# Inputs of an attention laid out as [d, token], the keys' maximum as a bias, and a new order of the attention's pieces

## The chip, the core and the metric

The kernel runs on one core of a Trainium2 chip. A core has five engines with a queue each: TensorE (PE; its weight loads are listed as PEld), VectorE (DVE), ScalarE (ACT), GpSimd (POOL) and SyncE (SP), which here issues all transfers. TensorE writes to PSUM; the others work on SBUF, and all but GpSimd also on PSUM. The metric is the device time of one execution in microseconds (us), lower is better.

## The reference

For 4 batches of 8 heads, 576 tokens and 64 dimensions per head, an attention with positive features, and then two feed-forward layers on the 2304 tokens:

```python
def phi(x):
    proj = np.einsum('bhsd,df->bhsf', x, w_phi)                      # 128 features
    proj = proj - np.max(np.abs(proj), axis=-1, keepdims=True)
    return np.concatenate([np.exp(proj), np.exp(-proj)], axis=-1)
q_p, k_p = (phi(q), phi(k))
kv = np.einsum('bhsf,bhsd->bhfd', k_p, v)
z = np.sum(k_p, axis=2)
num = np.einsum('bhsf,bhfd->bhsd', q_p, kv)
den = np.einsum('bhsf,bhf->bhs', q_p, z)[..., None] + 1e-06
attn = num / den
# x: the heads side by side, [2304, 512]
h = x @ w_in;    x = (h * sigmoid(h)) @ w_out          # 512 -> 2048 -> 512
h = x @ w2_in;   out = (h * np.cos(h)) @ w2_out
```

As the code computes it, the exponentials are exp(proj - max) and exp(-(proj - max)), where max is taken over the absolute values. The weights of the feed-forward layers are float64.

## The kernel before

Most products are made of float32 numbers split into two parts of fewer bits, hi and lo, and three matmuls: hi with hi, hi with lo, lo with hi. "Split" below means a cast to the short format (hi) and a subtraction (lo, the rest).

**The attention** works on eight groups n of four heads. Its pieces, as the tables START and PERIOD (L49, L55) name them:

- `load.k`, `load.q`, `load.v`: transfers. For k and q a main load of 512 KB and two small ones for the last 64 tokens of each head (the tails).
- `T.k.i`, `T.q.i` (L270, `transpose_in`): TensorE transposes a piece of k or q, [token, d], into PSUM (tile `tp`, two buffers); ScalarE casts it out of PSUM to hi, VectorE subtracts for lo.
- `phi.k.u`, `phi.q.u` (L290): products with w_phi into PSUM (tile `p`, two buffers); VectorE takes the maximum of absolute values (L304, `m`) and subtracts it (L306, `pm`, in SBUF). Unit 0 is the tails of the four heads, units 1 to 4 a head each.
- `kx.u` (L311): two exponentials on ScalarE, of +pm and -pm, for the keys.
- `qx.u` (L319): TensorE transposes pm of the queries (tile `t`, one buffer); ScalarE takes both exponentials (`e`), GpSimd casts them to hi (`qh`, L338).
- `ql.u.g` or `ql.u.v` (L341): the rest of the queries' exponentials, on GpSimd or VectorE.
- `kv.p.c.h` (L350): products of the keys' features with v and a column of ones; at the end ScalarE and VectorE split the sums. `num.p.i` (L373): the queries' features with these sums; ScalarE copies the result to `xn`.
- `inv.p` (L179): the inverses of the denominators, through a transfer to DRAM and back. `app.p` (L191): numerators times inverses, to x (`xy`), three multiplications on GpSimd.
- `piece`: a step of the conversion of a float64 weight (L99 to L126: a ScalarE step, three VectorE steps, two GpSimd steps for each of the first six weight tiles). `x`: x of the first tokens is split for the first layer.

Engines take their queues in the order in which the code issues them: the loop over n (L446) runs through PERIOD once per group, and a + or - at a piece's name shifts it by one group. One run through PERIOD is called a round here; the queries of a group meet the keys of the next one in it.

**The feed-forward layers** (L477, `moe`): for each layer, four groups of hidden columns by six blocks of 384 tokens, with the remaining weights converted beside the products. The change doesn't touch them, but for the row order of tokens in `store` (L567).

Of the kernel before, what the change touches and what calls it, by code (L numbers as in the profile page):

```python
# [158 lines left out]
class Norm:  # L159
    """Numerators over denominators, to x, [dm, token]."""  # L160
# [30 lines left out]
    def apply(self, n, p):  # L191
        nc, xy = self.nc, self.xy
# [7 lines left out]
        nc.gpsimd.tensor_mul(xy[rows, B * NJ + b // 2, c0:c0 + 2, at], t[rows, :, SM:S], r[rows, :, SM:S])  # L200


def attention(tc, q, k, v, w_phi, norm, pieces, then):
    nc = tc.nc
    W = D + 1
    with ExitStack() as ctx:
# [5 lines left out]
        kr, krt, qr, qrt = {}, {}, {}, {}  # L212

        def load_qk(n, src, main, tails, name):
            b, h0 = divmod(n, 2)
            h0 *= 4
            t = fp.tile([P, 4, NJ, D], F32, name=f"{name}r")
            u = fp.tile([P, 2, D], F32, name=f"{name}rt")
            for i in range(2):
                nc.sync.dma_start(u[64 * i:64 * i + 64], src[b, h0 + 2 * i:h0 + 2 * i + 2, SM:S, :].rearrange("h s d -> s h d"))  # L220
            nc.sync.dma_start(t, src[b, h0:h0 + 4, 0:SM, :].rearrange("h (p j) d -> p h j d", j=NJ))
            main[n], tails[n] = t, u
# [480 lines left out]
```

## Time and profile before

| | |
|---|---|
| median of 3 runs (lowest, highest) | 1051.86 us (1050.23, 1052.01) |
| span of the profiled execution, first to last instruction | 1048.8 us |
| busy in the span | PE 97%, DVE 68%, ACT 39%, POOL 35% |
| first product of the feed-forward layers | 228.6 us |
| starts of five rounds after another | 43.9, 71.8, 100.0, 128.4, 156.2 us |
| loads of k (512 KB), from issue to landing | 4.3 us (median) |
| loads of q (512 KB), from issue to landing | 4.1 us (median) |

The profiled execution's own time is not listed among the runs; its span is 3.1 us below their median. The shares are means over an attention of some 229 us and feed-forward layers of some 820 us, so the stretches have to be read apart. A round's start is taken here at the longest row of `kv` products (L363, 16 matmul rows), which stands once in each round.

### The profile page before, as it was taken

To read this page: it belongs to the slowest core of one execution; us is meant where nothing else is said; L and a number is where in the kernel's file an instruction comes from. 1 tells how busy PE (TensorE), PEld (TensorE's weight loads), DVE (VectorE), ACT (ScalarE), POOL (GpSimd) and SP (SyncE) were. 2 spreads that over 40 slices of the span, in tenths; PEclk is the share of its full clock that TensorE was granted. 3 is DMA by queue.
4 is the path that set the end of the run, shared out by engine and by line. 5 is a ranking of instruction groups with operands and counts; after the bars stand their busy time and mean duration, and the time that the engine had idled before them with its cause. 6 is when DMAs were issued, how large, how long until landed. Compare 5 with 4: busy or idle time off the path is not lost.

```text
span 1048.8 us, 15083 instructions
## 1 busy us (share of the span) xinstructions
PE 1019.1 (97%) x6000; PEld 972.5 (93%) x6000; DVE 711.9 (68%) x956; ACT 407.8 (39%) x664; POOL 369.4 (35%) x426
## 2 busy tenths in 40 slices
PE   7999999999999999999999999999999999999998
PEld 7989999989999999999999999899888988998997
DVE  6999999978544344544545567667677867786764
ACT  5655566544433222222223333444333333333332
POOL 3566666656122111201211024334434433343221
PEclk9999999999999999999999999999999999999999
DMA  4544333114111101110110111101110111100112
GB/s 118 139 112 112 99 105 81 47 40 129 41 41 46 55 22 61 41 41 21 61 48 34 41 41 42 40 21 61 41 41 21 61 40 41 27 34 1 61 57 63
DMA packets 62757, 58.33 MB, mean 56 GB/s; under 512 B 30560, under 2 KB 55264, under 8 KB 62688
## 3 DMA queue, kind: packets, MB, share of 16 engines
q1 hardware_dynamic: 62688, 57.38, 18.5%
q8 instruction: 47, 0.77, 0.3%
q14 instruction: 22, 0.18, 0.1%
HBM read 52.49 MB, written 4.79 MB: 55 GB/s over the span
## 4 chain that ended last, share of the span: by engine, by line
PE 61%; DVE 25%; POOL 7%; ACT 4%; issue 1%; DMA 1%; SPq 0%; POOLq 0%; ACTq 0%; DVEq 0%
PE h L509 24%; PE y L558 6%; PE y L560 6%; PE y L559 6%; DVE ql L346 4%; DVE tb L531 3%; DVE tb L530 3%; DVE tb L535 3%; PE kv L363 3%; POOL ta L529 2%; PE y L563 2%; PE y L564 2%; PE y L565 2%; DVE xy L589 2%; POOL gh L536 2%; DVE gl L538 2%
## 5 line engine op out<-in xcount | busy, mean ns | idle before, releaser
L509 PE MATMUL h<-xh,win_hi 128*128 128x384 f32 x768 | 259.1, 337 | 1.7 <-DVE tb L535 1.7
L509 PE MATMUL h<-xl,win_hi 128*128 128x384 f32 x768 | 258.8, 337 | 0.3 <-DVE xl L474 0.3
L509 PE MATMUL h<-xh,win_lo 128*128 128x384 f32 x768 | 258.7, 337 | 0.0
L521 DVE SCALAR_TENSOR_TENSOR ta<-ta,h 128x768 f32<-128x768 f32 x48 | 45.8, 953 | 177.7 <-ACT ta L520 177.7
L509 PEld LDWEIGHTS h<-xh,win_hi 128*128 128x128 f32 x768 | 144.2, 188 | 4.7 <-PE y L565 2.6
L509 PEld LDWEIGHTS h<-xl,win_hi 128*128 128x128 f32 x768 | 144.2, 188 | 2.4 <-DVE xl L474 0.6
L509 PEld LDWEIGHTS h<-xh,win_lo 128*128 128x128 f32 x768 | 144.2, 188 | 0.0
L532 ACT ACTIVATE tb<-tb 128x768 f32<-128x768 f32 x48 | 40.7, 847 | 239.0 <-DVE tb L531 239.0
L558 PE MATMUL y<-gh,wout_hi 128*128 128x384 f32 x384 | 129.5, 337 | 0.2 <-ACT xy L587 0.2
L560 PE MATMUL y<-gh,wout_lo 128*128 128x384 f32 x384 | 129.6, 337 | 0.0
L559 PE MATMUL y<-gl,wout_hi 128*128 128x384 f32 x384 | 129.4, 337 | 0.0
L520 ACT ACTIVATE ta<-h 128x768 f32<-128x768 f32 x48 | 39.0, 813 | 206.4 <-PE h L509 203.1
L563 PE MATMUL y<-wout_hi,gh 128*128 128x512 f32 x288 | 115.0, 399 | 3.3 <-ACT xy L587 1.8
L564 PE MATMUL y<-wout_lo,gh 128*128 128x512 f32 x288 | 114.4, 397 | 0.0
L565 PE MATMUL y<-wout_hi,gl 128*128 128x512 f32 x288 | 114.4, 397 | 0.0
L536 POOL TENSOR_SCALAR gh<-tb 128x768 fp32r<-128x768 f32 x48 | 46.9, 977 | 186.0 <-DVE tb L535 176.0
L538 DVE TENSOR_TENSOR gl<-tb,gh 128x768 fp32r<-128x768 f32 x48 | 75.4, 1570 | 34.3 <-POOL gh L536 34.3
L121 POOL TENSOR_SCALAR wout_hi<-wt 128x512 fp32r<-128x512 f32 x32 | 27.8, 869 | 200.3 <-DVE wt L118 171.1
L121 POOL TENSOR_SCALAR win_hi<-wt 128x512 fp32r<-128x512 f32 x32 | 21.6, 675 | 187.1 <-DVE wt L118 187.1
L589 DVE TENSOR_TENSOR xy<-y,xy 128x384 f32<-128x384 f32 (+1 forms) x126 | 70.8, 606 | 9.7 <-PE y L560 6.0
L535 DVE TENSOR_TENSOR tb<-tb,h 128x768 f32<-128x768 f32 x48 | 45.6, 951 | 46.7 <-ACT tb L533 46.2
L558 PEld LDWEIGHTS y<-gh,wout_hi 128*128 128x128 f32 x384 | 72.1, 188 | 0.5 <-ACT xy L587 0.5
(114 smaller groups left out, 2082.6 us busy)
## 6 DMA issues: line engine op xcount, KB each, us to landing
raw<-in_moe_w_in SPq DMA_DIRECT2D x32, 512.0 KB, 3.6
raw<-in_moe_w_out SPq DMA_DIRECT2D x32, 512.0 KB, 3.6
rb<-rd SPq DMA_DIRECT2D x16, 288.0 KB, 3.6
kr<-in_k SPq DMA_DIRECT2D x8, 512.0 KB, 4.3
qr<-in_q SPq DMA_DIRECT2D x8, 512.0 KB, 4.1
va<-in_v SPq DMA_DIRECT2D x32, 128.0 KB, 4.1
out<-xy SPq DMA_DIRECT2D x16, 256.0 KB, 2.2
krt<-in_k SPq DMA_DIRECT2D x16, 32.0 KB, 3.1
```

Of the source, the lines that this page charges most:

```text
L121: nc.gpsimd.tensor_scalar(hi, t.bitcast(F32), 1.0, 0.0, op0=ALU.mult, op1=ALU.add)
L509: nc.tensor.matmul(o, a[:, cs], x[t][:, :, c, :], start=first, stop=(c == NC - 1 and a is lo))
L535: nc.vector.tensor_mul(b, b, h)
L536: nc.gpsimd.tensor_scalar(hi, b, 1.0, 0.0, op0=ALU.mult, op1=ALU.add)
L538: nc.vector.tensor_sub(lo, b, hi.bitcast(F32))
L558: nc.tensor.matmul(o, wh[:, ds], hi[:, f, :], stop=False, **st)
L559: nc.tensor.matmul(o, wh[:, ds], lo[:, f, :], start=False, stop=False)
L560: nc.tensor.matmul(o, wl[:, ds], hi[:, f, :], start=False, stop=en)
L563: nc.tensor.matmul(o, hi[:, f, ds], wh, stop=False, **st)
L564: nc.tensor.matmul(o, hi[:, f, ds], wl, start=False, stop=False)
L565: nc.tensor.matmul(o, lo[:, f, ds], wh, start=False, stop=en)
L589: nc.vector.tensor_tensor(y, o, y, op=ALU.add)
```

## The change

- **Layout.** k and q reach the device as one array of 8 groups, [64 dimensions of two heads, tokens], tails first. One load of 576 KB per group takes the place of three. The transposes of the inputs and their tiles in PSUM are gone; `sp.k.i`, `sp.q.i` split the inputs straight from SBUF: a cast on the engine that the table names (D VectorE, A ScalarE, G GpSimd) and the rest on VectorE.
- **Keys.** VectorE still takes the maximum of `p`. GpSimd writes its negative (`nm`, 4 or 2 columns). ScalarE takes the exponentials out of PSUM, with `nm` and `m` as bias per token, 128 columns at a time: 8 (tail: 4) instructions instead of 2. VectorE's subtraction for the keys is gone; the tile `p` in PSUM is held until the exponentials are done.
- **Other engines.** The casts of the queries' exponentials go from GpSimd to ScalarE (two of them go to VectorE and two stay, in START). `ql.1` goes from VectorE to GpSimd, `app.1` from GpSimd to VectorE.
- **Buffers in PSUM.** `p` has three (was two), `t2` two (was one; `tp` had two).
- **Order.** START and PERIOD are rewritten. Tokens are assigned to tiles as j*128 + p instead of p*4 + j, which moves the rows of v's loads and of the output's stores.

The paths under `FULL`, an empty tuple, are not taken.

```diff
+PB, T2, KN = 3, 2, 3
 PERIOD = parse("""
-kx.1+ x.2+ num.1.1 x.3+ phi.k.2+ T.k.0++ phi.q.0+ num.1.0 x.4+ load.q++ kx.2+ num.1.2 x.5+ kv.0.0.0+ inv.0 phi.k.0++
...
+ql.4.D num.0.1 x.2+ num.0.2 num.0.3 kx.0+ num.1.0 kx.2+ sp.q.0.D+ x.4+ phi.k.3.A+ num.1.1 piece inv.0 num.1.2
...
         def load_qk(n, src, name):
+            t = fp.tile([P, GC], F32, name=f"{name}r")
+            nc.sync.dma_start(t, src[n])
...
-        def transpose_in(n, name, i):
...
-                    nc.tensor.transpose(ps[:, c * P:(c + 1) * P], src, ident)
...
-            nc.scalar.copy(hi, ps)
-            nc.vector.tensor_sub(lo, ps, hi.bitcast(F32))
...
+        def split_in(n, name, i, engine):
+            at = slice(0, P + SM) if i == 0 else slice(P + SM, GC)
+            hi, lo = xT[n, name, i] = [fp.tile([P, at.stop - at.start], F32R, name=f"{name}T_{part}{i}") for part in ("hi", "lo")]
+            src = raw[n, name][:, at]
+            cast(engine, hi, src)
+            nc.vector.tensor_sub(lo, src, hi.bitcast(F32))
...
             nc.vector.tensor_reduce(m, pv, axis=AX.X, op=ALU.max, apply_absolute_value=True)
+            if engine == "A":
+                nm = sp.tile([P, 2 * ns], F32, name="nm", bufs=3)
+                nc.gpsimd.tensor_scalar(nm, m, -1.0, 0.0, op0=ALU.mult, op1=ALU.add)
+                if name == "k":
+                    pm[n, name, u] = pv, m, nm
+                    return
...
-            nc.scalar.activation(t[:, 0], src, AF.Exp)
-            nc.scalar.activation(t[:, 1], src, AF.Exp, scale=-1.0)
+            for i in range(ns if m is not None else 0):
+                nc.scalar.activation(t[:, 0, i], src[:, i], AF.Exp, bias=nm[:, i:i + 1])
+                nc.scalar.activation(t[:, 1, i], src[:, i], AF.Exp, bias=m[:, i:i + 1], scale=-1.0)
...
-                    nc.gpsimd.tensor_scalar(hi, ev, 1.0, 0.0, op0=ALU.mult, op1=ALU.add)
+                        cast(engine, hi, ev)
...
-            nc.gpsimd.tensor_mul(xy[rows, b * NJ:(b + 1) * NJ, c0 + x, :], t[rows, x, 0:SM].rearrange("p (j n) -> p j n", n=P),
+            engine.tensor_mul(xy[rows, b * NJ:(b + 1) * NJ, c0 + x, :], t[rows, x, 0:SM].rearrange("p (j n) -> p j n", n=P),
```

Three places show how the instructions stand. VectorE before, in the middle of a round; `ql` are the rests of the queries, `m` a maximum, `pm` its subtraction, `wt` a weight, `r` the inverses:

```order
L346 TENSOR_TENSOR ql0_1896<-e_1955,qh0_1895 128x512
L346 TENSOR_TENSOR ql0_1896<-e_1958,qh0_1895 128x512
L183 TENSOR_SCALAR r_1993<-den_1890 128x9
L184 RECIPROCAL r_1993<-r_1993 128x9
L304 TENSOR_REDUCE m_2006<-p_1999 128x4
L306 TENSOR_TENSOR pm_2008<-p_1999,m_2006 128x512
L368 TENSOR_TENSOR kv0_lo_128<-kv_1846,kv0_hi_127 128x260
L118 SCALAR_TENSOR_TENSOR wt_1909<-ws_1907,wt_1909 128x512
L346 TENSOR_TENSOR ql0_1896<-e_1985,qh0_1895 128x512
L346 TENSOR_TENSOR ql0_1896<-e_1988,qh0_1895 128x512
```

VectorE now, at the end of a round and the start of the next; `xy` are multiplications of x, `qT_hi` and `qT_lo` the split of q:

```order
L397 TENSOR_TENSOR kv0_lo_122<-kv_1358,kv0_hi_121 128x260
L307 TENSOR_REDUCE m_1570<-p_1566 128x2
L374 TENSOR_TENSOR ql1_1408<-e_1541,qh1_1407 128x512
L374 TENSOR_TENSOR ql1_1408<-e_1542,qh1_1407 128x512
L397 TENSOR_TENSOR kv1_lo_124<-kv_1417,kv1_hi_123 128x4x65
L307 TENSOR_REDUCE m_1624<-p_1617 128x4
L205 TENSOR_TENSOR xy_63<-xn1_1295,rb_1340 64x4x128 x2
L208 TENSOR_TENSOR xy_63<-xn1_1295,rb_1340 64x2x64
L374 TENSOR_TENSOR ql1_1408<-e_1581,qh1_1407 128x512
L374 TENSOR_TENSOR ql1_1408<-e_1582,qh1_1407 128x512
L280 CAST qT_hi0_1691<-qr_1428 128x640
L290 TENSOR_TENSOR qT_lo0_1692<-qr_1428,qT_hi0_1691 128x640
```

Two of the round's rests, its multiplications of x, the last rests and the first split of q now stand close together, with only maxima and `kv_lo` between them; before, maxima with their subtractions, the inverses and a weight stood between two of the rests. On GpSimd, before, one round from the first casts of the queries' exponentials (`qh`) on:

```order
L338 TENSOR_SCALAR qh0_1101<-e_1161 128x512
L338 TENSOR_SCALAR qh0_1101<-e_1164 128x512
L197 TENSOR_TENSOR xy_63<-xn0_898,rb_1063 64x4x128 x2
L200 TENSOR_TENSOR xy_63<-xn0_898,rb_1063 64x2x64
L338 TENSOR_SCALAR qh0_1101<-e_1191 128x512
L338 TENSOR_SCALAR qh0_1101<-e_1194 128x512
L121 TENSOR_SCALAR win1_hi_66<-wt_1115 128x512
L338 TENSOR_SCALAR qh1_1103<-e_1229 128x512
L338 TENSOR_SCALAR qh1_1103<-e_1232 128x512
L338 TENSOR_SCALAR qh1_1103<-e_1251 128x512
L338 TENSOR_SCALAR qh1_1103<-e_1254 128x512
L197 TENSOR_TENSOR xy_63<-xn1_998,rb_1063 64x4x128 x2
```

GpSimd now, from the maximum of the keys' unit 4 on, where the code has `phi.k.4` (`nm` are the negated maxima, `win` a weight):

```order
L310 TENSOR_SCALAR nm_1439<-m_1437 128x4
L374 TENSOR_TENSOR ql0_1406<-e_1450,qh0_1405 128x512
L374 TENSOR_TENSOR ql0_1406<-e_1451,qh0_1405 128x512
L205 TENSOR_TENSOR xy_63<-xn0_1222,rb_1340 64x4x128 x2
L208 TENSOR_TENSOR xy_63<-xn0_1222,rb_1340 64x2x64
L129 TENSOR_SCALAR win2_hi_68<-wt_1331 128x512
L134 TENSOR_TENSOR win2_lo_69<-wt_1331,win2_hi_68 128x512
L310 TENSOR_SCALAR nm_1556<-m_1554 128x4
L310 TENSOR_SCALAR nm_1572<-m_1570 128x2
L310 TENSOR_SCALAR nm_1626<-m_1624 128x4
L310 TENSOR_SCALAR nm_1704<-m_1702 128x4
```

The casts of the queries' exponentials are gone from it; two rests of 512 columns, one set of multiplications of x and a weight stand in one piece, and the negated maxima of the keys' units 1, 0 and 2 behind it. On ScalarE, before, the exponentials of a group's queries (`e`, `et`) out of PSUM:

```order
L332 ACTIVATE et_1502<-t2_1495 128x256
L332 ACTIVATE et_1506<-t2_1495 128x256
L103 ACTIVATE ws_1510<-raw_720 128x512
L332 ACTIVATE e_1558<-t2_1553 128x512
L332 ACTIVATE e_1561<-t2_1553 128x512
L332 ACTIVATE e_1588<-t2_1583 128x512
L332 ACTIVATE e_1591<-t2_1583 128x512
L367 CAST kv0_hi_127<-kv_1449 128x260
```

ScalarE now, in the same place:

```order
L366 ACTIVATE e_1123<-t2_1118 128x512
L278 CAST qh0_1020<-e_1123 128x512
L366 ACTIVATE e_1124<-t2_1118 128x512
L278 CAST qh0_1020<-e_1124 128x512
L366 ACTIVATE e_1156<-t2_1151 128x512
L278 CAST qh1_1022<-e_1156 128x512
L366 ACTIVATE e_1157<-t2_1151 128x512
L278 CAST qh1_1022<-e_1157 128x512
L395 CAST kv0_hi_121<-kv_973 128x260
```

Behind each exponential stands the cast of its result.

## Rows read from the trace of the kernel before

**Rows 1.** Busy time by stretch: from:to, its us, each engine's busy us (instructions), clock, DMA.
```profile
0.00:8.10 8.10, 1.98 (x8) 1.72 (x9) 1.34 (x5) 1.94 (x3) 2.69 (x22) 1.00 0.46 127
0.00:228.62 228.62, 208.54 (x1680) 205.42 (x1681) 210.52 (x339) 133.94 (x298) 135.38 (x206) 0.97 0.36 96
128.43:156.23 27.80, 25.94 (x212) 25.83 (x212) 27.27 (x45) 16.62 (x37) 18.15 (x26) 0.94 0.39 106
156.23:182.60 26.37, 24.36 (x205) 23.93 (x205) 25.50 (x42) 15.81 (x37) 17.00 (x23) 1.00 0.36 91
260.00:1048.80 788.80, 779.73 (x4151) 737.06 (x4149) 476.78 (x592) 260.32 (x348) 218.45 (x207) 1.00 0.13 41
```

**Rows 2.** Line 346, attention: count, duration ns min/median/max, first and last start.
```profile
L346 DVE TENSOR_TENSOR ql<-e,qh x62: 677/922/2987, 26.4 to 226.5; 128x512 fp32r<-128x512 f32 x62
```

**Rows 3.** Timeline of VectorE, one round: start us, us, line, operation, tiles, shapes.
```profile
132.69 3.78 DVE L346 TENSOR_TENSOR ql<-e,qh 128x512 fp32r<-128x512 f32 x2
...
146.94 0.28 DVE L285 TENSOR_TENSOR kT_lot<-tp,kT_hit 128x128 fp32r<-128x128 f32 x1
...
148.46 1.33 DVE L346 TENSOR_TENSOR ql<-e,qh 128x512 fp32r<-128x512 f32 x2
149.71 0.68 DVE L285 TENSOR_TENSOR qT_lom<-tp,qT_him 128x512 fp32r<-128x512 f32 x1
150.31 0.67 DVE L304 TENSOR_REDUCE m<-p 128x4 f32<-128x512 f32 x1
151.02 0.69 DVE L306 TENSOR_TENSOR pm<-p,m 128x512 f32<-128x512 f32 x1
```

**Rows 4.** Timeline of GpSimd, same round.
```profile
132.55 2.50 POOL L197 TENSOR_TENSOR xy<-xn,rb 64x512 f32<-64x512 f32 x2
...
147.35 1.29 POOL L126 TENSOR_TENSOR win_lo<-wt,win_hi 128x512 fp32r<-128x512 f32 x1
```

**Rows 5.** VectorE's groups, 0 to 229 us: count, busy us, mean ns, idle before.
```profile
L346 DVE TENSOR_TENSOR ql<-e,qh 128x512 fp32r<-128x512 f32 x62 | 70.5, 1178 | 0.2 <-POOL qh L338 0.2
...
L306 DVE TENSOR_TENSOR pmt<-p,m 128x256 f32<-128x256 f32 x16 | 6.8, 424 | 0.5
...
L107 DVE TENSOR_SCALAR wt<-raw 128x512 int32<-128x512 int32 x6 | 2.7, 442 | 0.0
```

**Rows 6.** GpSimd's groups, 0 to 229 us.
```profile
L338 POOL TENSOR_SCALAR qh<-e 128x512 fp32r<-128x512 f32 x64 | 44.2, 711 | 11.7 <-ACT e L332 11.6
L197 POOL TENSOR_TENSOR xy<-xn,rb 64x512 f32<-64x512 f32 x28 | 40.6, 1468 | 1.9 <-DMA rb<-rd 1.5
...
L346 POOL TENSOR_TENSOR ql<-e,qh 128x512 fp32r<-128x512 f32 x2 | 2.5, 1278 | 0.0
```

**Rows 7.** Timeline of TensorE at the start.
```profile
6.56 1.97 PE L278 MATMUL tp<-ident,kr 128*128 128x128 f32 x8 [2.14 <-DMA kr<-in_k]
8.18 0.56 PE L299 MATMUL p<-wphi,kT_hit 128*128 128x256 f32 x1
```

**Rows 8.** Timeline of TensorE in that round; in brackets the idle time before.
```profile
138.64 1.09 PE L324 MATMUL t<-ident,pm 128*128 128x128 f32 x4 [1.86 <-DVE pm L306]
...
149.00 0.60 PE L278 MATMUL tp<-ident,kr 128*128 128x128 f32 x4
149.35 0.37 PE L299 MATMUL p<-wphi,qT_hit 128*128 128x256 f32 x1
```

**Rows 9.** ScalarE's groups, 0 to 229 us.
```profile
L315 ACT ACTIVATE kp<-pm 128x512 f32<-128x512 f32 x32 | 20.3, 634 | 8.5 <-DVE pm L306 8.3
...
L284 ACT CAST kT_him<-tp 128x512 fp32r<-128x512 f32 x16 | 9.4, 589 | 5.4 <-PE tp L278 5.2
...
L315 ACT ACTIVATE kpt<-pmt 128x256 f32<-128x256 f32 x8 | 3.4, 425 | 1.5 <-DVE pmt L306 1.5
...
L284 ACT CAST kT_hit<-tp 128x128 fp32r<-128x128 f32 x8 | 2.1, 265 | 2.5 <-PE tp L280 2.4
```

**Rows 10.** Busy time and granted clock just behind TensorE's wait.
```profile
138.00:142.00 4.00, 3.36 (x19) 3.39 (x20) 3.96 (x7) 1.48 (x3) 2.49 (x3) 0.58 0.35 97
```

More of the change, by code (lines that the diff above doesn't have):

```diff
@@ L210, in attention, with load_qk @@
         pp = ctx.enter_context(tc.tile_pool(name="at_ps", bufs=1, space=PSUM))
[L212 to L222, printed above, removed]
+        raw = {}
+        def load_qk(n, src, name):
+            t = fp.tile([P, GC], F32, name=f"{name}r")
+            nc.sync.dma_start(t, src[n])
+            raw[n, name] = t
         def load_v(n):
@@ L255, in attention @@
                 nc.gpsimd.memset(t[64 * x:64 * x + 64, i % 2, c:c + 1], 1.0)
-        kvs = [[sp.tile([P, 2, 2, M], F32R, name=f"kv{i}_{part}") for part in ("hi", "lo")] for i, M in enumerate((W, P))]
+        kvs = [[sp.tile([P, 2, 2, M], F32 if i in FULL else F32R, name=f"kv{i}_{part}") for part in (("all",) if i in FULL else ("hi", "lo"))]
+               for i, M in enumerate((W, P))]
         for t in kvs[1]:
@@ new lines, in attention, with cast @@
+        engines = {"D": nc.vector, "A": nc.scalar, "G": nc.gpsimd}
+        def cast(engine, out, src):
+            if engine == "A":
+                nc.scalar.copy(out, src)
+            elif engine == "D":
+                nc.vector.tensor_copy(out, src)
+            else:
+                nc.gpsimd.tensor_scalar(out, src, 1.0, 0.0, op0=ALU.mult, op1=ALU.add)
+        def split_in(n, name, i, engine):
[4 more added lines that the diff above has]
+            nc.vector.tensor_sub(lo, src, hi.bitcast(F32))
@@ new lines, in q_exp @@
+            for i in full:
+                for c in range(2):
+                    src = ps[:, i, :].rearrange("p (x s) -> p x s", x=2) if u == 0 else ps.rearrange("p a s -> p (a s)")
+                    nc.scalar.activation(qh[n, i][:, c, :, SM:S] if u == 0 else qh[n, i][:, c, x, 0:SM], src, AF.Exp, scale=1.0 - 2.0 * c)
+            parts = rests[n, u] = []
+            if u and full or len(full) == 2:
+                return
+            es = [sp.tile([P, ns, P], F32, name="et" if u == 0 else "e", bufs=2 if u == 0 else 4) for _ in range(2)]
@@ L341, in q_rest @@
         def q_rest(n, u, engine):
-            for c in range(2):
-                for i in range(2 if u == 0 else 1):
-                    lo, ev, hi = rests.pop((n, u, c, i))
-                    engine.tensor_sub(lo, ev, hi.bitcast(F32))
+            for _, ev, hi, lo in rests.pop((n, u)):
+                engine.tensor_sub(lo, ev, hi.bitcast(F32))
         kvp = {}
@@ L402, in step @@
                 return then(front)
-            key = (n, name, *arg)[:3] if name == "ql" else (n, name, *arg)
+            key = (n, name, *(a for a in arg if a not in engines))
             if key in done or not 0 <= n < NQ:
@@ L424, in step @@
             elif name == "ql":
-                q_rest(n, arg[0], nc.gpsimd if arg[1] == "g" else nc.vector)
+                q_rest(n, arg[0], engines[arg[1]])
             elif name == "kv":
@@ L439, in step @@
             elif name == "app":
-                norm.apply(n, *arg)
+                norm.apply(n, arg[0], engines[arg[1]])
         done.update({(0, "load", "k"), (0, "load", "q")})
@@ L692 @@
     for name in ("q", "k", "v", "w_phi", "moe_w_in", "moe_w_out", "moe2_w_in", "moe2_w_out"):
-        a = np.ascontiguousarray(inputs[name])
+        a = inputs[name]
+        if name in ("q", "k"):
+            x = np.asarray(a).reshape(2 * B, 4, S, D)
+            main = x[:, [0, 2, 1, 3], :SM].reshape(2 * B, 4, 2, 2, P, D).transpose(0, 3, 5, 1, 2, 4).reshape(2 * B, P, 8 * P)
+            tail = x[:, :, SM:].reshape(2 * B, 2, 2, S - SM, D).transpose(0, 2, 4, 1, 3).reshape(2 * B, P, P)
+            a = np.concatenate([tail, main], axis=2)
+        a = np.ascontiguousarray(a)
         if a.dtype == np.float64:
```

121 lines of the change are left out of this document (64 added, 57 removed).

## The prediction, written before the changed kernel ran

> **What bounds the kernel now.** I cut the span into stretches first, then read one round of the attention in the timelines, then the groups of instructions. The busy shares of the whole span are means over two parts with different limits. From 260 us to the end TensorE is busy for 779.7 of 788.8 us: the two feed-forward layers are TensorE's, and the change leaves their work as it is (only the order of the output rows differs) [rows 1]. The attention is the other part: the first product of the feed-forward layers starts at 228.6 us, and up to there VectorE is busy for 210.5 us [rows 1]. In one round (128.43 to 156.23 us) VectorE is busy for 27.27 of 27.80 us, TensorE for 25.94, ScalarE for 16.62, GpSimd for 18.15 [rows 1]. So a round is as long as VectorE's list, with TensorE close behind and ScalarE at 60%.
>
> Why VectorE's list is that long is the main reading. The same instruction, the rest of the queries' exponentials (L346, 128x512, both inputs in SBUF), takes from 677 to 2987 ns [rows 2]. Two of them take 1.33 us where GpSimd is almost idle, and 3.78 us where it multiplies x beside them [rows 3, 4]. Subtractions of the same size with one input in PSUM never show this: 0.67 to 0.69 us each [rows 3]. So VectorE pays for GpSimd's company, and only with instructions whose inputs both lie in SBUF; I call them pair instructions. 62 of them at a mean of 1178 ns instead of 677 [rows 5] are 31.1 us of waiting in VectorE's 210.5; without it the list is 179.4 us.
>
> **The change, on VectorE.** Durations in a row overlap by about 0.08 us, so I count start to start: 0.60 for a 512 subtraction, 0.71 for a maximum, 0.20 for a tail of 128, 0.62 for an undisturbed pair instruction (148.46 to 149.71 for two) [rows 3], and 0.34 for a tail of 256 [rows 5].
> Removed over eight rounds: the rests of the transposed inputs, 32 x 0.60 + 16 x 0.20 = 22.4; the keys' subtraction of the maximum, 32 x 0.60 + 8 x 0.34 = 21.9; 14 of 62 rests of the queries, 14 x 0.62 = 8.7. Together 53.0 us.
> Added: the rests of the inputs straight from SBUF, now pair instructions of 512 and 640 elements, 16 x 0.62 + 16 x 0.75 = 21.9; 18 casts, priced like L107 (442 ns for 512 [rows 5]; 0.43, and 0.53 for 640), 8.5; half of the multiplications of x, 14 x 0.62 + 7 x 0.27 = 10.6. Together 41.0 us.
> The list without waiting becomes 179.4 - 53.0 + 41.0 = 167.4 us.
>
> **The waiting for GpSimd** is the term that decides. Per round there are about 17 such instructions (6 rests of queries, 4 of inputs, 2 casts, 3 multiplications, 2 of a weight's conversion) instead of 10. Bound from above: each waits 0.50 us, the mean of before, 8.5 us a round. Bound from below: hardly any, 1.2 us a round. The new order decides between them. GpSimd loses its 64 large casts of exponentials (0.71 us each), 32 small ones and half of the x (1.47 each) and gains two casts and two rests of 1.28 a round [rows 6]; by these rows its list goes from about 17 to about 11.5 us a round. Its long piece (two rests, three multiplications of x, a weight) now stands beside VectorE's maxima and subtractions out of PSUM; VectorE's two later rests of queries, its multiplications of x and the first split of q stand where GpSimd has only the small negated maxima. What still meets: a weight's step and k's second split beside four small rests (3 x 0.3), a weight's merge beside a 1.3 us multiplication (0.8), the first rests after a weight's two GpSimd steps (1.0), the splits of k and q behind their own casts (0.4), the inverses (0.4). That is 3.5 us a round, 24.5 over seven, nearer to the lower bound because most pair instructions now have no long neighbour.
> The Trainium skill ("SBUF — State Buffer", section "SBUF: two separate sides") says that VectorE and GpSimd share one pair of ports as an exclusive lock, which a VectorE instruction with two SBUF inputs or in a two-port mode takes for its whole duration. The trace agrees with that for two inputs (1.33 against 3.78 us for the same two); that a cast from SBUF takes the lock too, no run here shows. By that rule this change is suspect, since it gives VectorE more instructions that need the lock; what that would cost is rival C below, priced from rows alone.
>
> **Start and idle time.** VectorE idles for 18.1 of the 228.6 us, 6.8 of them before 8.1 us [rows 1]. The first transposes wait for k until 6.56 us and the first product with w_phi stands at 8.18 [rows 7]. Now k is the first transfer in SP's queue, and a cast (some 0.7) and a rest (0.75) take the place of eight transposes; the transfer is 576 KB in place of 512. I take 1.5 us off. The other idle time I keep: a second and third buffer in PSUM remove waits, but the other engines now come closer. Idle: 16.6 us.
> Sum: 167.4 + 24.5 + 16.6 = 208.5 us in place of 228.6, so 20.1 us less.
>
> **Edits that I cost at nothing, and their cover.** TensorE loses 144 transposes, some 13 us (four take 0.35 start to start [rows 8]), which lie behind VectorE's list. ScalarE: it loses the casts of the inputs (32 x 0.50 + 16 x 0.19 = 19.0) and the keys' large exponentials (64 x 0.54 + 16 x 0.33 = 39.8) [rows 9], and gains 60 casts of 512 and 32 of 128 elements (60 x 0.50 + 32 x 0.19 = 36.1) and 288 exponentials of 128 columns with a bias. No row has such an exponential; the nearest is the 128-column cast out of PSUM, 0.27 us long [rows 9], 0.19 start to start. So ScalarE goes from 133.9 [rows 1] to between 166 and 189 us, below 208 but no longer idle. The 40 negated maxima on GpSimd stand between a maximum and its exponentials; those of three units queue behind the multiplications of x and a weight (some 5 us), but their exponentials come half a round later. If that cover were gone, ScalarE and the PSUM buffer that the keys now hold until their exponentials are done would wait by those 5 us a round. SP loses 32 small loads; the loads of k and q have one buffer each and stand behind the last read of it, some 7 us ahead of use where a load of 512 KB lands after about 4 (the table of the page's figures).
>
> **Rivals.**
> *A, the forecast: VectorE still bounds, waits 2 to 6 us a round.* 198 to 218 us; the likeliest is 208.5.
> *B, the waiting nearly goes, TensorE bounds.* TensorE's 208.5 us of attention [rows 1] less 13 of transposes and less some 5 of slow clock: in this round TensorE waited 1.86 us for VectorE [rows 8] and in the next 4 us the granted clock was 0.58, so mostly at the lower of its levels (1.2 GHz); rounds with such a stretch took 27.8 us, without 26.4 [rows 1, 8, 10]. 190 plus 7 to 10 of start and end gives 199 us, 29 less: 1022.
> *C, slower: the port.* If each of the 17 instructions waits 0.50 us, VectorE has 167.4 + 59.5 + 16.6 = 243.5 us, 14.9 more than now: 1067. It turns from gain to loss at (228.6 - 16.6 - 167.4) / 7 = 6.4 us a round, 0.38 each. Against it: the order above.
> *D, ScalarE bounds.* With 111.2 us of other work and 18 of idle time, small exponentials of 0.27 start to start give 207 us, of 0.33 give 224: 1047. Short waits on bias and maxima would do this.
> *E, no change:* the removed work was covered. Against it stands a VectorE that is busy for 98% of a round.
>
> **How the numbers follow.** The profiled execution's span is 1048.8 us; the median of the runs shown, 1051.86, is 3.1 us above it, and I carry that over. A: 1048.8 - 20.1 + 3.1 = 1031.8, call it 1032. Chances: A 0.55 (1021 to 1041), B 0.17 (1014 to 1023), D 0.13 (1040 to 1050), C 0.12, E 0.03. The range 1015 to 1044 leaves out C, E, the upper part of D and the edge of B, some 0.2. A measurement can tell about 0.2%, 2 us, from no change. Faster: A, B and nearly all of D, 0.84; within 0.2%: 0.04; slower: C, 0.12.
>
> **What would show it.** Right: the first product of the feed-forward layers at about 208 us, rounds of 24 to 25.5 us with VectorE busy for all but 1 us of them, the rests of the queries at a mean under 0.95 us, small exponentials of 0.25 to 0.3 us, ScalarE at 80 to 90% in the attention, feed-forward layers unchanged. Wrong: pair instructions with a mean above 1.1 us (C); ScalarE without idle time and VectorE waiting for TensorE or ScalarE in each round (D); a clock at the lower level in most rounds; or a feed-forward part that changes in length.

## The result, and the profile after

| | before | after |
|---|---|---|
| median (lowest, highest) | 1051.05 us (1047.64, 1052.01), 4 runs | 1023.52 us (1022.47, 1024.13), 4 runs |
| ratio, 95% interval | | 0.9751 [0.9728, 0.9773] |
| span of the profiled execution | 1048.8 us | 1021.3 us |
| first product of the feed-forward layers | 228.6 us | 202.3 us |
| a round, mean of six | 27.5 us | 24.0 us |

The change makes the kernel 27.5 us faster; the forecast was 20. The time lies inside the range, 8 us below its likeliest value. All but 1 us of it is in the attention: from the first product of the feed-forward layers to the end of the span it is 820.2 us before and 819.0 after.

Busy time by stretch of the kernel after (from:to, its us, then busy us and instructions of PE, PEld, DVE, ACT, POOL, granted clock, DMA share, GB/s), which answers [rows 1]:

```profile
0.00:202.30 202.30, 189.17 (x1536) 184.11 (x1536) 179.82 (x310) 187.43 (x552) 102.67 (x162) 1.00 0.41 108
120.17:144.87 24.70, 23.48 (x195) 22.70 (x193) 24.04 (x40) 24.19 (x71) 15.11 (x20) 1.00 0.37 98
...
260.00:1021.30 761.30, 751.49 (x3998) 708.88 (x3996) 464.09 (x578) 247.87 (x331) 213.78 (x204) 1.00 0.13 41
```

VectorE's 210.5 us have become 179.8. But read across the second row: in a round of 24.70 us ScalarE is busy for 24.19, VectorE for 24.04, TensorE for 23.48. Before, VectorE had 98% of a round, TensorE 93% and ScalarE 60%. The clock is 1.00 all through the attention, where [rows 10] showed 0.58.

The rests of the queries, VectorE's row of their line, which answers [rows 2]: the longest is 1757 ns in place of 2987, the median 685 in place of 922.

```profile
L374 DVE TENSOR_TENSOR ql<-e,qh x48: 676/685/1757, 24.7 to 198.6; 128x512 fp32r<-128x512 f32 x48
```

VectorE's timeline in one round (start us, us, line, operation, tiles, shapes), which answers [rows 3]:

```profile
119.85 2.40 DVE L374 TENSOR_TENSOR ql<-e,qh 128x512 fp32r<-128x512 f32 x2
...
122.84 1.28 DVE L374 TENSOR_TENSOR ql<-e,qh 128x512 fp32r<-128x512 f32 x2
...
126.62 1.29 DVE L374 TENSOR_TENSOR ql<-e,qh 128x512 fp32r<-128x512 f32 x2
127.83 0.49 DVE L280 CAST qT_hi<-qr 128x640 fp32r<-128x640 f32 x1
128.35 0.83 DVE L290 TENSOR_TENSOR qT_lo<-qr,qT_hi 128x640 fp32r<-128x640 f32 x1
...
130.03 0.17 DVE L191 TENSOR_SCALAR r<-den 128x9 f32<-128x9 f32 x1
...
138.99 0.69 DVE L319 TENSOR_TENSOR pm<-p,m 128x512 f32<-128x512 f32 x1
139.60 1.74 DVE L126 SCALAR_TENSOR_TENSOR wt<-ws,wt 128x512 int32<-128x512 int32 x1
141.27 1.25 DVE L191 TENSOR_SCALAR r<-den 128x9 f32<-128x9 f32 x1
```

GpSimd's timeline in the same round, which answers [rows 4]:

```profile
120.11 1.58 POOL L134 TENSOR_TENSOR win_lo<-wt,win_hi 128x512 fp32r<-128x512 f32 x1
...
125.21 0.62 POOL L310 TENSOR_SCALAR nm<-m 128x4 f32<-128x4 f32 x1 [1.64 <-DVE m L307]
129.87 0.30 POOL L310 TENSOR_SCALAR nm<-m 128x4 f32<-128x4 f32 x1 [4.03 <-DVE m L307]
...
137.05 2.50 POOL L374 TENSOR_TENSOR ql<-e,qh 128x512 fp32r<-128x512 f32 x2
139.51 2.97 POOL L205 TENSOR_TENSOR xy<-xn,rb 64x512 f32<-64x512 f32 x2
```

Two tables side by side: where GpSimd has only negated maxima (122.8 to 130 us), the rests and the split of q run at their bare 0.5 to 0.8 us each. The two rests at 119.85, beside a weight's step on GpSimd, take 2.40 us. GpSimd's two rests at 137.05 meet maxima and subtractions out of PSUM, which don't wait. Its multiplications of x at 139.51 meet two victims, the merge of a weight (1.74 us) and the inverses' first step (1.25 us for 9 columns, 0.17 at 130.03). VectorE's groups from 0 to 205 us, which answer [rows 5] (count, busy us, mean ns, idle before):

```profile
L374 DVE TENSOR_TENSOR ql<-e,qh 128x512 fp32r<-128x512 f32 x48 | 34.1, 751 | 0.2
L191 DVE TENSOR_SCALAR r<-den 128x9 f32<-128x9 f32 x15 | 9.8, 652 | 0.2
...
L126 DVE SCALAR_TENSOR_TENSOR wt<-ws,wt 128x512 int32<-128x512 int32 x6 | 8.8, 1464 | 0.0
...
L290 DVE TENSOR_TENSOR kT_lo<-kr,kT_hi 128x512 fp32r<-128x512 f32 x8 | 6.7, 834 | 0.3
...
L280 DVE CAST qT_hi<-qr 128x640 fp32r<-128x640 f32 x8 | 3.9, 489 | 0.0
```

Waiting, counted against undisturbed rows: rests 48 x (751 - 676) = 3.6 us; inverses 15 x (652 - 170) = 7.2; merges 6 x (1464 - 693) = 4.6 (693 is their mean in u3_swap, below); the rests of k 8 x (834 - 684) = 1.2, with 684 the mean of q's of that size; some 1 for the casts. Together about 18 us.

The group of ScalarE's exponentials with the negated maximum as bias over the same stretch, and a piece of its timeline, which answer [rows 9]:

```profile
L332 ACT ACTIVATE kp<-p,nm 128x128 f32<-128x128 f32 x128 | 54.8, 430 | 0.6 <-POOL nm L310 0.5
```

```profile
124.00 0.37 ACT L332 ACTIVATE kp<-p,nm 128x128 f32<-128x128 f32 x1
124.26 0.36 ACT L333 ACTIVATE kp<-p,m 128x128 f32<-128x128 f32 x1
```

A small exponential lasts 0.36 to 0.43 us but the next starts 0.25 us later, and 0.25 is what it costs. This group waited 0.5 us for its bias in the whole attention; the group of the tails waited 2.8 us, once, at the start (until 8.2 us). TensorE's start, which answers [rows 7]: the first product with w_phi stands at 5.72 us in place of 8.18.

```profile
5.72 0.55 PE L302 MATMUL p<-wphi,kT_hi 128*128 128x256 f32 x1 [5.72 <-DVE wphi L269]
```

### The profile page after: what moved, and what is told of

It is laid out like the page before. It is cut to its first block, busy times and chain, and to the rows that moved or that the text cites. A ratio compares the mean times of both kernels' runs of the same rounds, so it can differ in the third digit from the quotient of the medians.

```text
span 1021.3 us, 14938 instructions
## 1 busy us (share of the span) xinstructions
PE 998.1 (98%) x5856; PEld 950.1 (93%) x5856; DVE 681.5 (67%) x925; ACT 460.4 (45%) x917; POOL 335.7 (33%) x380
## 4 chain that ended last, share of the span: by engine, by line
PE 61%; DVE 10%; POOL 5%; ACT 3%; issue 1%; POOLq 0%; ACTq 0%; DVEq 0%
PE h L541 30%; PE y L592 7%; PE y L590 7%; PE y L591 7%; PE y L595 4%; PE y L596 4%; PE y L597 4%; DVE tb L563 2%; DVE tb L562 2%; DVE tb L567 2%; POOL ta L561 2%; POOL gh L568 2%; POOL wout_lo L134 1%; DVE gl L570 1%; DVE xy L621 1%; ACT tb L564 1%
## 5 line engine op out<-in xcount | busy, mean ns | idle before, releaser
L553 DVE SCALAR_TENSOR_TENSOR ta<-ta,h 128x768 f32<-128x768 f32 x48 | 45.8, 954 | 179.8 <-ACT ta L552 179.8
L592 PEld LDWEIGHTS y<-gh,wout_lo 128*128 128x128 f32 x384 | 72.1, 188 | 0.0
```

Source lines behind the costliest of these rows:

```text
L592: nc.tensor.matmul(o, wl[:, ds], hi[:, f, :], start=False, stop=en)
```

## The experiments

Theory: VectorE's list with its waits for GpSimd sets the attention (the forecast). Rivals after the result: ScalarE has become the bound; or the three lists are tied, and the new order is what keeps them from waiting for each other. Ratios are against the kernel before, medians beside them. Edits are shown against the kernel after where nothing else is said.

**One engine relieved at a time.** Three kernels take work from one engine each, and one from two. In s1_act the keys' exponentials are two large instructions with one bias column, which belongs to the first head alone.

```diff
-            for i in range(ns if m is not None else 0):
-                nc.scalar.activation(t[:, 0, i], src[:, i], AF.Exp, bias=nm[:, i:i + 1])
-                nc.scalar.activation(t[:, 1, i], src[:, i], AF.Exp, bias=m[:, i:i + 1], scale=-1.0)
+            if m is not None:
+                nc.scalar.activation(t[:, 0], src, AF.Exp, bias=nm[:, 0:1])
+                nc.scalar.activation(t[:, 1], src, AF.Exp, bias=m[:, 0:1], scale=-1.0)
```

> The changed kernel, with the keys' exponentials taken as two instructions of 512 columns per unit (256 for the tails) that use the first column of the bias for all columns; so the exponentials of all but one group of columns have the wrong shift, everything else is as in the changed kernel. ScalarE's list loses per round 36 x 0.25 - 8 x 0.50 - 2 x 0.30 = 4.4 us. Theory VectorE (its list sets the round, ScalarE only looks full): 1020 to 1025 us, as the changed kernel (1023.5). Theory ScalarE (busy for 24.1 of 24.6 us in a round): rounds fall to VectorE's list of 23.1 to 24.0 us or below, 1012 to 1018. Theory tie (three lists of nearly the same length): 1018 to 1022.

In s2_dve the maximum is taken over half of the features.

```diff
-            nc.vector.tensor_reduce(m, pv, axis=AX.X, op=ALU.max, apply_absolute_value=True)
+            nc.vector.tensor_reduce(m, pv[:, :, 0:F // 2], axis=AX.X, op=ALU.max, apply_absolute_value=True)
```

> The changed kernel, with the maximum taken over the first half of the features only; so the maximum is too small for some tokens, everything else is as in the changed kernel. VectorE's list loses per round 8 x 0.27 + 2 x 0.13 = 2.4 us. Theory VectorE: up to 2.4 us less per round, 1005 to 1012 us. Theory ScalarE: 1020 to 1025. Theory tie: 1018 to 1022.

In s3_pe the third product of the numerators is left out.

```diff
-                        nc.tensor.matmul(o, kh, b, start=False, stop=False)
-                        nc.tensor.matmul(o, kl, a, start=False, stop=(c == 1))
+                        nc.tensor.matmul(o, kh, b, start=False, stop=(c == 1))
```

> The changed kernel without the third product of the numerators (rest of kv with the queries' high part); everything else is as in the changed kernel. TensorE's list loses 16 x 0.13 = 2.1 us per round. Theories VectorE and ScalarE: 1020 to 1025 us. If TensorE set the round: 1007 to 1013. Theory tie: 1019 to 1023.

s4_act_dve has the first two edits together.

> Both of the first two edits at once: one bias column for two large exponentials of the keys, and the maximum over half of the features; the rest as in the changed kernel. Theory VectorE: as with the edit on VectorE alone, 1005 to 1012 us. Theory ScalarE: as with the edit on ScalarE alone, or some us less. Theory tie: more than the sum of the two alone, until TensorE's list (23.3 us busy in rounds of 24.4) stops it, 1008 to 1015.

Measured: s1_act 1021.22 us (0.973 [0.9705, 0.9756]), s2_dve 1020.61 (0.9722 [0.97, 0.9745]), s3_pe 1019.81 (0.9716 [0.9692, 0.9739]), s4_act_dve 1013.91 (0.966 [0.9639, 0.9681]). Busy time up to the first product of the feed-forward layers, in this order (columns as above), one kernel each:

```profile
0.00:200.30 200.30, 186.67 (x1536) 183.94 (x1536) 179.21 (x309) 160.73 (x344) 104.56 (x162) 1.00 0.41 109
```

```profile
0.00:199.80 199.80, 188.44 (x1536) 184.86 (x1536) 163.22 (x309) 186.77 (x552) 106.63 (x162) 1.00 0.42 110
```

```profile
0.00:197.40 197.40, 178.36 (x1409) 169.27 (x1409) 179.53 (x310) 186.64 (x552) 103.81 (x162) 1.00 0.41 111
```

```profile
0.00:192.90 192.90, 184.50 (x1537) 183.26 (x1537) 162.26 (x310) 159.76 (x344) 107.42 (x162) 1.00 0.42 114
```

27 us off ScalarE bring 2.3 us of time, 17 off VectorE 2.9, 11 off TensorE 3.7. These three differ from each other by about as much as the runs of one kernel scatter (s3_pe from 1018.3 to 1021.2), so they don't rank the engines. The first two together bring 9.6, where their sum is 5.2, and that is clear of the scatter. Neither engine was the bound alone: when one is relieved, the others still fill the round. In s2_dve VectorE loses 16.6 us of work and idles for 36.6 us in place of 22.5. In s4_act_dve TensorE is busy for 184.5 of 192.9 us and would be next. So the attention is tied; the forecast's single bound no longer holds after the change.
The Trainium skill ("Perfetto Trace Analysis", section "Identifying the Most-Contended Engine") says to find the engine of highest occupancy and to improve that one first, and that TensorE's busy share is no good measure of how near its limit it is. Here the shares name no single engine: in the round above ScalarE has the highest and TensorE the lowest, but up to the first product of the feed-forward layers TensorE has the highest (189.2 us, ScalarE 187.4, VectorE 179.8), and relieving any one of them gave 2 to 4 us. So the first half of the rule is of little use in this tie, and no run here tests the second.

**One part undone.** u1_keys takes the keys' subtraction back to VectorE and their exponentials back to two large instructions.

```diff
-ql.4.D num.0.1 x.2+ num.0.2 num.0.3 kx.0+ num.1.0 kx.2+ sp.q.0.D+ x.4+ phi.k.3.A+ num.1.1 piece inv.0 num.1.2
+ql.4.D num.0.1 x.2+ num.0.2 num.0.3 kx.0+ num.1.0 kx.2+ sp.q.0.D+ x.4+ phi.k.3.D+ num.1.1 piece inv.0 num.1.2
...
```

> The changed kernel with one part undone: VectorE subtracts the keys' maximum again, into SBUF, and ScalarE takes two large exponentials per unit. VectorE gains 4 x 0.60 + 0.34 = 2.7 us a round, ScalarE loses 4.4, GpSimd loses the negated maxima. Theories VectorE and tie: the round grows with VectorE's list, up to 8 x 2.7 = 22 us, 1038 to 1046 us. Theory ScalarE: 1016 to 1021.

Measured: 1045.07 us (0.996 [0.9946, 0.9974]), 21.5 slower than after. 32 subtractions at 0.60 and 8 at 0.34 are 21.9 us, the prediction's price for them. A round, and four microseconds of it:

```profile
103.50:130.80 27.30, 24.74 (x187) 23.71 (x187) 26.11 (x45) 18.94 (x42) 11.37 (x13) 0.94 0.39 108
103.00:107.00 4.00, 4.00 (x24) 4.00 (x22) 3.48 (x6) 3.58 (x7) 3.21 (x4) 0.57 0.03 3
```

VectorE leads again, ScalarE is down to 69%, and each round has a stretch at the lower clock. Without the keys' bias four fifths of the change's gain are gone. That the loss equals VectorE's price to 0.4 us is in part chance: up to the first product of the feed-forward layers (223.0 us) VectorE is busy for 24.9 us more than in the kernel after and idles for 4.2 us less, and TensorE waits for the queries' `pm` for 11.0 us between 45 and 215 us.

u2_casts takes the casts of the queries' exponentials back to GpSimd.

```diff
-x.1+ phi.q.0.D+ kv.0.0.0+ sp.k.0.G++ sp.q.1.G+ kx.3+ phi.q.1.D+ num.1.3 qx.0.A+ kv.1.0.0+ piece ql.0.G+ x.3+
+x.1+ phi.q.0.D+ kv.0.0.0+ sp.k.0.G++ sp.q.1.G+ kx.3+ phi.q.1.D+ num.1.3 qx.0.G+ kv.1.0.0+ piece ql.0.G+ x.3+
...
```

> The changed kernel with the casts of the queries' exponentials back on GpSimd. ScalarE loses 4.5 us a round, GpSimd gains 6. Theory port (VectorE's instructions with both inputs in SBUF wait for GpSimd): the rests of the queries go from a mean of 0.75 us to 0.95 to 1.2 us, VectorE's list grows by 2 to 5 us a round, 1032 to 1055 us. Without that: 1016 to 1021, as with less work on ScalarE.

Measured: 1057.03 us (1.007 [1.0055, 1.0085]), 2 us above the expected range and 0.7% slower than before. VectorE's group of the queries' rests, up to 236 us:

```profile
L374 DVE TENSOR_TENSOR ql<-e,qh 128x512 fp32r<-128x512 f32 x48 | 48.7, 1055 | 14.7 <-POOL qh L282 14.5
```

Two prices in one row: the rests wait inside (1055 ns in place of 751, 14.6 us in all) and VectorE stands idle before them for 14.5 us. TensorE then waits for VectorE's `kv_lo` behind them, 19.0 us in five waits between 45 and 195 us, and the clock is 0.93 in the mean up to the first product of the feed-forward layers.

u3_swap takes `ql.1` back to VectorE and `app.1` back to GpSimd.

```diff
-load.q++ phi.k.4.A+ sp.k.1.D++ qx.1.A+ x.6+ phi.q.2.D+ kx.4+ ql.1.G+ app.0.G phi.q.3.D+ piece kv.0.0.1+
+load.q++ phi.k.4.A+ sp.k.1.D++ qx.1.A+ x.6+ phi.q.2.D+ kx.4+ ql.1.D+ app.0.G phi.q.3.D+ piece kv.0.0.1+
...
-ql.3.D+ qx.4.A+ load.k+++ x.0+ kv.1.1.0+ kv.1.1.1+ num.0.0+ load.v++ phi.k.2.A++ kx.1++ app.1.D
+ql.3.D+ qx.4.A+ load.k+++ x.0+ kv.1.1.0+ kv.1.1.1+ num.0.0+ load.v++ phi.k.2.A++ kx.1++ app.1.G
```

> The changed kernel with ql.1 back on VectorE and app.1 back on GpSimd, at their new places in the order. By the lists alone VectorE loses 0.3 us a round and GpSimd gains 0.4: 1021 to 1025 us. Theory port: GpSimd's multiplications now stand beside VectorE's last rests and the first split of q, and ql.1 adds two instructions that can wait: 1.5 to 3 us a round, 1033 to 1045 us.

Measured: 1037.22 us (0.9881 [0.9865, 0.9898]), 13.7 slower than after. VectorE's groups up to 236 us, then a piece of its timeline and of GpSimd's:

```profile
L290 DVE TENSOR_TENSOR qT_lo<-qr,qT_hi 128x640 fp32r<-128x640 f32 x8 | 12.4, 1556 | 0.3
L280 DVE CAST qT_hi<-qr 128x640 fp32r<-128x640 f32 x8 | 10.4, 1304 | 0.0
```

```profile
132.48 1.28 DVE L374 TENSOR_TENSOR ql<-e,qh 128x512 fp32r<-128x512 f32 x2
133.68 1.58 DVE L280 CAST qT_hi<-qr 128x640 fp32r<-128x640 f32 x1
```

```profile
133.30 3.11 POOL L205 TENSOR_TENSOR xy<-xn,rb 64x512 f32<-64x512 f32 x2
```

The cast of q has one input, and takes 1.58 us beside GpSimd's multiplication in place of 0.49. That is the point that the prediction had to leave open. The Trainium skill ("SBUF — State Buffer", section "SBUF: two separate sides") counts among VectorE's instructions that need the shared pair those in a two-port mode beside those with two SBUF inputs; this row and the inverses' step (0.17 against 1.25 us) agree that inputs are not the whole test, though no run shows the mode itself.

**Parts alone in the old order.** b1_casts is the kernel before with the queries' casts on ScalarE.

```diff
-                    nc.gpsimd.tensor_scalar(hi, ev, 1.0, 0.0, op0=ALU.mult, op1=ALU.add)
+                    nc.scalar.copy(hi, ev)
```

> One part of the change alone, in the kernel before: the casts of the queries' exponentials on ScalarE instead of GpSimd, nothing else. GpSimd loses 64 x 0.71 + 32 x 0.32 = 55 us, ScalarE gains 38 to 41 on 134. Theory port: the rests of the queries go from a mean of 1.18 us to 0.8 to 1.0, VectorE's list loses 10 to 20 us: 1030 to 1041 us. If the place of the casts doesn't matter: 1047 to 1053.

Measured: 1045.84 us (0.9963 [0.9951, 0.9975]), much less than expected. Busy time up to the first product, and two of VectorE's groups:

```profile
0.00:224.76 224.76, 208.99 (x1681) 200.83 (x1681) 199.74 (x339) 177.41 (x395) 86.36 (x110) 1.00 0.38 98
```

```profile
L346 DVE TENSOR_TENSOR ql<-e,qh 128x512 fp32r<-128x512 f32 x62 | 60.1, 1010 | 0.0
...
L285 DVE TENSOR_TENSOR qT_lom<-tp,qT_him 128x512 fp32r<-128x512 f32 x16 | 11.0, 687 | 5.2 <-ACT qT_him L284 5.2
```

VectorE's busy time falls by 10.8 us, nearly all of it (10.4) in the rests' waiting for GpSimd, and its idle time rises by 6.9 (25.0 against 18.1), most of it in waits for a fuller ScalarE. The difference, 3.9 us, is what the first product gains. So about a third of what leaves VectorE's list shows in the time, with 43 us more on ScalarE.

l1_layout has the layout alone: the old order, engines and numbers of buffers, and no transposes of the inputs. Its edit against the kernel after:

```diff
-PB, T2, KN = 3, 2, 3
+PB, T2, KN = 2, 1, 3
...
+kx.1+ x.2+ num.1.1 x.3+ phi.k.2.D+ sp.k.0.A++ phi.q.0.D+ num.1.0 x.4+ load.q++ kx.2+ num.1.2 x.5+ kv.0.0.0+ inv.0 phi.k.0.D++
...
```

> One part of the change alone: inputs as [d, token] (no transposes, the splits of the inputs from SBUF, casts on ScalarE), with the order, the engines and the PSUM buffers of the kernel before (two for p, one for t2). VectorE's list without waiting stays as before (22 us leave, 22 us come), TensorE loses 13 us, and 4 more instructions a round with both inputs in SBUF can wait for GpSimd. Theory VectorE with the port: 1046 to 1066 us against 1051 before. Theory TensorE (its transposes set the rounds before): 1034 to 1042.

Measured: 1061.07 us (1.0107 [1.0086, 1.0128]): removing 144 transposes, and splitting the inputs straight from SBUF, alone makes the kernel 1.1% slower. l2_layout_casts adds the casts on ScalarE and the new numbers of buffers. Its edit against l1_layout:

```diff
-PB, T2, KN = 2, 1, 3
+PB, T2, KN = 3, 2, 3
...
-sp.k.1.A++ num.1.3 x.6+ qx.0.G+ piece phi.q.1.D+ ql.0.G+ phi.q.2.D+ kv.1.0.0+ kv.0.0.1+ piece qx.1.G+ phi.q.4.D+ app.0.G
+sp.k.1.A++ num.1.3 x.6+ qx.0.A+ piece phi.q.1.D+ ql.0.G+ phi.q.2.D+ kv.1.0.0+ kv.0.0.1+ piece qx.1.A+ phi.q.4.D+ app.0.G
...
```

> Layout as [d, token], the casts on ScalarE and the PSUM buffers of the changed kernel (three for p, two for t2), in the order of the kernel before, with the keys' maximum subtracted on VectorE and app on GpSimd as before. If new engines and buffers do it without the new order and the keys' bias: 1025 to 1035 us. If these two carry the rest of the gain (VectorE's list is 22 us longer without the keys' bias, and GpSimd's multiplications stand beside VectorE's rests): 1040 to 1055.

Measured: 1059.35 us (1.0091 [1.0071, 1.0111]), above both expectations. Two of VectorE's groups up to 236 us:

```profile
L289 DVE TENSOR_TENSOR qT_lo<-qr,qT_hi 128x512 fp32r<-128x512 f32 x8 | 7.4, 930 | 7.9 <-ACT qT_hi L277 7.9
...
L306 DVE TENSOR_REDUCE m<-p 128x2 f32<-128x256 f32 x16 | 6.7, 420 | 14.5 <-PE p L303 14.4
```

The rests are down to a mean of 877 ns, yet VectorE idles: it waits for TensorE, and TensorE for the splits of q (13.3 us in ten waits between 45 and 200 us), which stand in the old places of the transposes, directly ahead of their products.

o1_order is the last step: every edit of the change, and the same instructions on each engine in a round, but START and PERIOD in the order of before.

```diff
...
-x.1+ phi.q.0.D+ kv.0.0.0+ sp.k.0.G++ sp.q.1.G+ kx.3+ phi.q.1.D+ num.1.3 qx.0.A+ kv.1.0.0+ piece ql.0.G+ x.3+
...
+kv.1.1.1+ load.k+++ num.0.0+ kx.0++ ql.3.D+ phi.k.4.A++ num.0.1+ load.v++ num.0.2+ x.0++ kx.3++ kx.4++
+phi.k.1.A++ ql.4.D+ app.1.D num.0.3+ x.1++ sp.q.0.D++ piece
```

> The changed kernel with all of its edits (layout, keys' bias on ScalarE, queries' casts on ScalarE, ql.1 on GpSimd, app.1 on VectorE, the engines of the splits in PERIOD, three and two buffers in PSUM), but START and PERIOD in the order of the kernel before. Each engine gets the same instructions as in the changed kernel, in another order. Theory 1 (the gain is in the engines' lists being nearly equal, whatever their order): 1023 to 1028 us. Theory 2 (lists that are nearly equal need an order in which each piece's input is done in time; where it is not, the waiting engine loses what no other has to spare, and TensorE's waits bring stretches at the lower clock): 1035 to 1055 us, the rests of the queries at a mean over 850 ns, TensorE waiting over 1 us at a time in each round, and stretches with a granted clock below 1. Between 1028 and 1035 both have a share.

Measured: 1057.05 us (1.0069 [1.0054, 1.0084]), just above the upper case, 33.5 us slower than after. The rests have a mean of 734 ns, so that part of theory 2 failed: they hardly wait. Other instructions wait instead: the inverses' first step has a mean of 1350 ns (652 after), the multiplications of x 1106 (687 after). One round and the stretch from its end on, then a piece of TensorE's timeline there and of VectorE's:

```profile
98.96:127.56 28.60, 25.64 (x194) 24.25 (x194) 24.74 (x39) 23.60 (x69) 12.80 (x18) 0.92 0.37 103
126.00:132.00 6.00, 6.00 (x29) 6.00 (x30) 2.47 (x7) 2.92 (x11) 0.88 (x2) 0.57 0.32 99
```

```profile
120.93 0.30 PE L420 MATMUL num<-qh,kv_hi 128*128 128x288 f32 x1
121.07 0.29 PE L421 MATMUL num<-ql,kv_hi 128*128 128x288 f32 x1
...
125.18 0.55 PE L301 MATMUL p<-wphi,qT_hi 128*128 128x256 f32 x1 [2.63 <-DVE qT_hi L279]
...
126.57 0.44 PE L421 MATMUL num<-ql,kv_hi 128*128 128x288 f32 x1
126.81 0.44 PE L422 MATMUL num<-qh,kv_lo 128*128 128x288 f32 x1
```

```profile
120.73 1.28 DVE L373 TENSOR_TENSOR ql<-e,qh 128x512 fp32r<-128x512 f32 x2
122.02 2.28 DVE L204 TENSOR_TENSOR xy<-xn,rb 64x512 f32<-64x512 f32 x2
...
124.54 0.49 DVE L279 CAST qT_hi<-qr 128x640 fp32r<-128x640 f32 x1
```

VectorE multiplies x while TensorE needs the split of q that stands behind. The two multiplications take 2.28 us in place of the 1.29 of the kernel after: GpSimd's subtraction for a weight, 1.72 us from 121.43 on, stands beside them, so about 1 us of the delay is waiting for GpSimd and the rest is the order. TensorE is idle for 2.63 us, and the matmuls after that last 0.44 us in place of 0.29 and start 0.24 us apart in place of 0.14. Over the round its busy time is 25.64 us against 23.48 in the kernel after. The same work in a round, in another order, makes the difference: by where a product's input stands in its queue, and by which of VectorE's instructions meet GpSimd's. In this table the multiplications of x stand ahead of the split because `app.1`, moved to VectorE, kept its old place; another mixture of the two orders might cost less, and none was tried.

**A try at more.** The two victims of GpSimd's long piece suggested i1_balance: the merge of a weight earlier, and the casts of the tails' exponentials on GpSimd instead of ScalarE.

```diff
-x.1+ phi.q.0.D+ kv.0.0.0+ sp.k.0.G++ sp.q.1.G+ kx.3+ phi.q.1.D+ num.1.3 qx.0.A+ kv.1.0.0+ piece ql.0.G+ x.3+
-load.q++ phi.k.4.A+ sp.k.1.D++ qx.1.A+ x.6+ phi.q.2.D+ kx.4+ ql.1.G+ app.0.G phi.q.3.D+ piece kv.0.0.1+
+x.1+ phi.q.0.D+ kv.0.0.0+ sp.k.0.G++ sp.q.1.G+ kx.3+ phi.q.1.D+ num.1.3 qx.0.G+ kv.1.0.0+ piece piece ql.0.G+ x.3+
+load.q++ phi.k.4.A+ sp.k.1.D++ qx.1.A+ x.6+ phi.q.2.D+ kx.4+ ql.1.G+ app.0.G phi.q.3.D+ kv.0.0.1+
```

> The changed kernel with two more shifts: the third step of a weight's conversion directly behind the second, ahead of GpSimd's long piece of work, and the four small casts of the tails' exponentials on GpSimd, which idles for 3 us there. VectorE loses 1.1 us of waiting in each of six rounds, ScalarE 0.8 us in each round. Theory tie: both lists get shorter, TensorE's doesn't, 1017 to 1021 us. Theory that one of the two lists sets the round: 1014 to 1018. If GpSimd's longer list delays the rests: 1023 to 1028.

Measured: 1029.53 us (0.9808 [0.9788, 0.9828]), 6 slower than after and above all three expectations. The merge is back at 0.69 us and the inverses' step at 0.40, but GpSimd's timeline and one row of VectorE's show the price:

```profile
139.46 1.76 POOL L282 TENSOR_SCALAR qh<-et 128x128 fp32r<-128x128 f32 x4 [2.91 <-ACT et L366]
...
141.95 2.12 POOL L374 TENSOR_TENSOR ql<-et,qh 128x128 fp32r<-128x128 f32 x4
144.04 0.19 POOL L310 TENSOR_SCALAR nm<-m 128x4 f32<-128x4 f32 x1
```

```profile
147.48 0.69 DVE L307 TENSOR_REDUCE m<-p 128x4 f32<-128x512 f32 x1 [1.74 <-PE p L304]
```

A negated maximum now stands behind the tails on GpSimd; ScalarE waits for such biases (6.5 us between 47 and 195 us, in the kernel after none in that stretch), and VectorE for products in `p` (14.8 us against 5.5), as if the buffers that the keys hold came free too late. That cause is argued, not shown: the two edits were not tried singly. In one round TensorE's clock falls as well (0.57 from 120 to 124 us). No version tried that does all of the work beats the changed kernel.

## Why the prediction came out as it did

**The direction held, and the reading that VectorE's pair instructions wait for GpSimd.** u1_keys, u2_casts and u3_swap each put back one part and lose 21.5, 33.5 and 13.7 us. That VectorE's list alone set the rounds before is not shown: b1_casts took 10.8 us off it, with 43 us more on ScalarE, and gained 3.9. After the change, rival A's "VectorE still bounds" is wrong: VectorE is busy for all but 0.7 us of the round above, as forecast, and yet 16.6 us off its list bring 2.9.

**The sum, term by term.** List without waiting: forecast 167.4 us, measured 179.8 - 18 = 162; about 2.7 of the 5 are waits of the inverses in the kernel before (14 at a mean of 365 ns, alone 170), which the sum took for work, since it looked for waits only in pair instructions. Waits: forecast 24.5 us, measured 18. Their place was half right: the rests, feared for most, cost 3.6 us, and the merge and the inverses, priced at 0.8 and 0.4 a round, cost 0.8 and 1.0. Idle time: forecast 16.6 us, measured 202.3 - 179.8 = 22.5. Together 202.3 against 208.5: 6 of the 8 us; the rest is the feed-forward part (1.2) and the carry from span to median, 2.2 us after the change where 3.1 was taken (0.9).

**The step that failed is "the other idle time I keep".** It was given no working, and it is the term that the order decides: o1_order has the same work in a round and idles for 50.2 us on VectorE (238.6 to the first product, 188.4 busy). The prediction used the order only to place waits for GpSimd. In o1_order the busy time holds waiting too, 8.6 us more than after. The forecast came out near because this order holds the idle time down, not because of a reason that the prediction gave: in this term it was luck.

**TensorE and the clock** were costed at nothing, as lying behind VectorE. They were not free: without the transposes' 13 us TensorE is still at 95% of a round, and its waits in u1_keys, u2_casts and o1_order come with the losses. The slow clock that rival B priced at some 5 us is gone (1.00), but that price is not borne out. It was read from two rounds, 27.8 us with a slow stretch and 26.4 without; an earlier round of the kernel before took as long without one:

```profile
43.88:71.84 27.96, 25.38 (x212) 24.62 (x212) 26.68 (x44) 16.44 (x37) 17.80 (x26) 1.00 0.40 106
```

The short round has less work, 42 instructions of VectorE against 44 and 45, and in b1_casts, at a clock of 1.00, TensorE is busy for 209.0 us, no less than before. The 1023.5 us lie next to B's 1022, though by a tie and not by TensorE alone.

**ScalarE** came to 187.4 us, at the top of the forecast's 166 to 189, with 0.25 us for a small exponential: rival D set in at 0.27. "No longer idle" understated it; at 93% of the attention and 98% of a round it is one of three bounds, and the expected 80 to 90% was wrong. The cover named for the negated maxima held (3.3 us of waiting, all of it before 10 us); in i1_balance, with the tails' casts ahead of one, ScalarE waits 6.5 us for them. GpSimd's list, forecast at about 11.5 us a round, is 15.1 in the round above: the sum left out the negated maxima, 2.8 us in five.

**The start** gained 2.5 us where 1.5 was taken. Rival C did not come: the rests' mean is 0.75 us, under the 0.95 that was set. What stays open is how much of the gain belongs to the order and how much to the edits: in the old order the casts alone bring 4 us, the layout alone costs 11, and all of the edits together cost 7; the new order without the edits was not tried.

## What to carry to other kernels

When a change relieves the fullest engine and fills two others to 95% or more of a round, a sum of one list's work is only the lower end; look in the tables for the instruction that another engine needs next, and at what stands ahead of it in its queue. An order that was tuned for one distribution of work can turn a good redistribution into a loss, so try the two together. Price an edit on the engine where it sits, then ask which engines are nearly as full (here 98, 97 and 95% of a round): there gains don't add up singly, and relieving two engines brought nearly twice the sum of both.
